# Kernel: packed attention into a mixture of experts, where the opening is re-ordered (second half of the first batch's tokens, identity matmuls, second batch's attention)

## The chip, the cores and the metric

The kernel runs on one core of one Trainium2 chip. The metric is the device time of one execution in microseconds; lower is better. The median of three runs of the kernel before is 1284.36 us, from 1283.30 to 1284.87.

## What is computed

Attention in two steps, eight batches of eight heads, 576 positions and 64 columns a head: 32 packed queries `p` attend to `k` and `v`, then `q` attends to what they found. The result is the input of a mixture of four experts with given weights.

```python
p_packed = sm_attn(p, k, v)            # (8, 8, 32, 64)
out = sm_attn(q, p_packed, p_packed)   # (8, 8, 576, 64)
x = out.transpose(0, 2, 1, 3).reshape(4608, 512)
p = domain_probs / (domain_probs.sum(-1, keepdims=True) + 1e-09)
for e in range(4):
    h = np.maximum(x @ w1[e], 0.0)     # 512 -> 1024
    y += p[:, e:e + 1] * (h @ w2[e])   # 1024 -> 512
```

## The kernel before, in words

**Tokens.** The attention weights of the second step have only 32 columns a head, so `x @ w1` is computed as (weights `a2`) times (`p_packed @ w1`). `pack_unit` (L176) makes `p_packed` of a batch and leaves it in `ppbd`: scores on TensorE, row maximum on VectorE, exponential on ScalarE, transposes with the identity, product with `v`. The weights `a2`, transposed, are the tokens `xh` and `xl`, a high and a low part in fp32r: ScalarE writes `xh` (a rounding copy), GpSimd writes `xl` (the remainder). For the first batch `tok_halves` (L292) does this for positions 0 to 287 and 288 to 575 apart, each for two groups g of four heads; for all others `tok_unit` (L256) does whole rows. In `tok_halves`, `shifted` subtracts the maximum and calls for the exponential, and `normed` sums, inverts, multiplies, transposes (five VectorE instructions) and makes `xh` and `xl`.

**Chunks and units.** The 4 x 1024 hidden columns are eight chunks `ch` of 512. A unit is one chunk of one batch: `units` lists (0, 0, 0), (0, 1, 0), (0, 1, 1), (0, 0, 1) and so on as (pair of batches, chunk, batch), so units 0 and 1 are the first batch's and unit 2 the first of the second batch. `g_form` (L359) makes `ghl`, the product of `ppbd` with a piece of `w1`, for a chunk (8 matmul calls a batch). `mm1_group(u, kh, c)` (L403) makes one quarter block of the hidden layer of unit u: token half c, hidden half kh, named a11, a12, a21, a22 (`f"a{c + 1}{kh + 1}"`), 24 x 128x288 matmuls for two blocks; one VectorE SCALAR_TENSOR_TENSOR does the ReLU and the weight.

**Seven products.** The second layer is a 2 x 2 block product done with seven products in the order `ORDER` (a11, s3, s1, s2, a22, s4, a12). `mm1_group` forms the sums s1 to s4 on VectorE; `s_operand` (L453) makes the high part of an operand `st` on ScalarE and the low part on GpSimd; a12's own operand `stl` has its low part made on VectorE, out of PSUM. `product` (L516) is 12 matmuls; its result is copied to `acc` by ScalarE (first chunk of a batch) or added by VectorE. `t_form` (L485) makes the weights `tt` of a chunk out of two pieces `rw0` and `rw1` of `w2`: four subtractions on GpSimd (in place in `rw`), high parts on ScalarE, low parts on GpSimd. The next chunk's pieces are loaded into the same tiles by SyncE once the last low part was read.

**Memory for sums.** PSUM holds four tiles `dbl` of two banks; nearly every step on TensorE takes one, so a tile that is read late holds up a later step.

**What sets the order.** Engines take their instructions in a fixed order. A scheduler puts it together when the kernel is built; the code constrains it: `together` and `on_pe` (L96 to L118) chain TensorE, `InOrder` keeps VectorE and GpSimd in the order of the code while `on` is set (from L659 to L683), and `Behind` puts attention work of VectorE (`avec`) behind the latest block sum. `avec.on` also keeps matmuls of other kinds behind the latest product (L99), from unit 1 on.

**The opening.** L641 to L684 are the code before the units: first batch's attention, `halves` in steps, `g_form` of chunk 0, weights of chunk 0 in steps (`forms`), second batch's score matmuls (`packs[2:]`), then blocks a11 and a12 (`mm1_group(0, 0, 0)`, `(0, 1, 0)`), which need the first half of the tokens, and a22 and a21, which need the second. The loop over units (L708) then issues, after each product i, the operands, `g_form`, blocks of the next unit, and one or two steps of `second_batch` (L688), which was drained before unit 1.

## Time and profile before

| | |
|---|---|
| median of three runs | 1284.36 us (1283.30 to 1284.87) |
| the profiled execution | 1284.25 us |
| its span, first to last instruction | 1282.5 us |
| outside the span | 1.75 us |
| TensorE (PE) busy | 1247.8 us, 97% of the span |
| VectorE (DVE) busy | 926.9 us, 72% |
| GpSimd (POOL) busy | 729.5 us, 57% |
| ScalarE (ACT) busy | 501.5 us, 39% |
| mean granted clock of TensorE | 0.996 |

How to read the views: a row of the timeline gives start and duration in us, the engine, the line, the operation, what it writes and reads, the count, and in square brackets the idle time before it with what ended that. A row that stands for several instructions runs from the first one's start to the last one's end. PE are matmuls, PEld weight loads, SPq the issue of transfers by SyncE. In a row of the windows the stretch comes first, then its length, the busy time of PE, PEld, DVE, ACT and POOL with their counts, the granted clock, the share of the transfer engines and GB/s. A group's row ends with the count, busy time, mean ns of one, and the idle time before.

### The profile page before, as it was taken

How to read it: one execution, taken by the hardware profiler on the slowest of the kernel's cores; microseconds unless marked ns; L12 is line 12 of the kernel's file. 1: busy time of each engine (PE TensorE's matmuls, PEld its weight loads, DVE VectorE, ACT ScalarE, POOL GpSimd, SP SyncE). 2: the span in 40 equal slices, each digit the busy share in tenths (PEclk: the TensorE clock that was granted, in tenths of full speed). 3: DMA queues.
4: the chain of work that ended last, by engine and by line, in shares of the span. 5: the costliest groups of instructions: out<-in, count | busy, mean ns of one | idle time of the engine just before them, and what ended most of it. 6: DMA issues, size and time to landing. Idle time of an engine off the chain costs nothing.

```text
span 1282.5 us, 26863 instructions
## 1 busy us (share of the span) xinstructions
PE 1247.8 (97%) x10720; PEld 1165.6 (91%) x10720; DVE 926.9 (72%) x1398; ACT 501.5 (39%) x850; POOL 729.5 (57%) x528
## 2 busy tenths in 40 slices
PE   5899999999999999999999999999999999999997
PEld 3789998988989999999999999999999999999997
DVE  6675776697975677889685666788768467766677
ACT  2555544344445343334235433343333533333331
POOL 3877868778774343455466343454457445434545
PEclk9899999999999999999999999999999999999999
DMA  9675656425465444554454554433445443344422
GB/s 339 237 259 172 231 200 242 170 102 209 160 222 181 159 157 165 158 168 152 132 171 153 180 191 160 157 118 117 158 153 198 151 136 118 129 135 158 125 66 75
DMA packets 86220, 213.71 MB, mean 167 GB/s; under 512 B 8784, under 2 KB 27344, under 8 KB 86096
## 3 DMA queue, kind: packets, MB, share of 16 engines
q1 hardware_dynamic: 85424, 211.85, 49.4%
q8 instruction: 86, 1.41, 0.5%
q14 instruction: 38, 0.31, 0.1%
q10 hardware_dynamic: 672, 0.15, 0.1%
HBM read 173.09 MB, written 38.87 MB: 165 GB/s over the span
## 4 chain that ended last, share of the span: by engine, by line
PE 82%; POOL 5%; DVE 5%; DMA 3%; issue 3%; ACT 1%; POOLq 0%; SPq 0%; DVEq 0%; ACTq 0%
PE dbl L104 76%; PE dbl L112 5%; POOL st L68 3%; DVE acc L68 1%; POOL acc L68 1%; DVE a L68 1%; POOL tt L68 1%; DMA rw<-in_w 1%; DMA pnd<-ablk 1%; PE dbl L107 1%; DVE ghl L68 1%; DMA pbt<-pnd 1%; POOL rw L68 0%; DVE dbl L68 0%; DVE sblk L68 0%
## 5 line engine op out<-in xcount | busy, mean ns | idle before, releaser
L104 PE MATMUL dbl<-st,tt 128*128 128x288 f32 x4608 | 665.9, 296 | 11.0 <-POOL st L68 6.5
L104 PEld LDWEIGHTS dbl<-st,tt 128*128 128x128 f32 x4608 | 622.9, 188 | 46.5 <-issue 27.2
L68 POOL TENSOR_TENSOR st<-sblk,st 128x576 fp32r<-128x576 f32 x256 | 373.3, 1468 | 391.2 <-ACT st L139 364.3
L104 PE MATMUL dbl<-xh,ghl 128*128 128x288 f32 x2048 | 414.4, 295 | 0.0
L68 DVE TENSOR_TENSOR acc<-dbl,acc 128x576 f32<-128x576 f32 x391 | 293.3, 751 | 87.3 <-PE dbl L104 85.0
L104 PEld LDWEIGHTS dbl<-xh,ghl 128*128 128x128 f32 x2048 | 328.8, 189 | 0.2 <-DVE ghl L68 0.2
L104 PE MATMUL dbl<-xl,ghl 128*128 128x288 f32 x1024 | 303.0, 296 | 6.4 <-POOL xl L68 5.7
L139 ACT CAST st<-sblk 128x576 fp32r<-128x576 f32 x256 | 166.5, 674 | 310.7 <-DVE sblk L68 253.7
L68 POOL TENSOR_TENSOR st<-ablk,st 128x576 fp32r<-128x576 f32 x128 | 185.2, 1447 | 53.3 <-ACT st L139 51.1
L104 PEld LDWEIGHTS dbl<-xl,ghl 128*128 128x128 f32 x1024 | 193.1, 189 | 9.3 <-POOL xl L68 6.4
L68 DVE SCALAR_TENSOR_TENSOR dbl<-dbl,pbt 128x576 f32<-128x576 f32 x128 | 97.8, 764 | 83.3 <-PE dbl L104 77.0
L139 ACT CAST st<-ablk 128x576 fp32r<-128x576 f32 x128 | 86.2, 674 | 151.1 <-PE dbl L104 125.4
L68 DVE SCALAR_TENSOR_TENSOR ablk<-dbl,pbt 128x576 f32<-128x576 f32 x128 | 96.4, 753 | 49.6 <-PE dbl L104 46.7
L68 DVE TENSOR_TENSOR ghl<-dbl,ghl 128x512 fp32r<-128x512 f32 x128 | 85.3, 687 | 54.3 <-ACT ghl L139 54.3
L104 PE MATMUL dbl<-stl,tt 128*128 128x288 f32 x768 | 113.0, 296 | 1.0 <-DVE acc L68 1.0
L104 PEld LDWEIGHTS dbl<-stl,tt 128*128 128x128 f32 x768 | 104.4, 188 | 3.2 <-DVE acc L68 2.6
L139 ACT CAST ghl<-dbl 128x512 fp32r<-128x512 f32 x128 | 72.0, 588 | 60.5 <-DVE ghl L68 50.8
L68 POOL TENSOR_TENSOR tt<-rw,tt 128x512 fp32r<-128x512 f32 x56 | 71.9, 1300 | 33.4 <-ACT tt L139 33.3
L68 DVE TENSOR_TENSOR stl<-dbl,stl 128x576 fp32r<-128x576 f32 x64 | 48.3, 755 | 38.4 <-ACT stl L139 38.4
L112 PE MATMUL dbl<-wraw,ppbd 64*32 64x512 f32 x1024 | 67.5, 595 | 0.8 <-DMA wraw<-in_w 0.8
L440 ACT COPY sblk<-dbl 128x576 f32<-128x576 f32 x64 | 41.0, 641 | 66.5 <-DVE sblk L68 66.5
L533 ACT COPY acc<-dbl 128x576 f32<-128x576 f32 x56 | 35.9, 640 | 49.9 <-PE dbl L104 49.8
(63 smaller groups left out, 695.4 us busy)
## 6 DMA issues: line engine op xcount, KB each, us to landing
tt<-td SPq DMA_DIRECT2D x175, 512.0 KB, 4.2
wraw<-in_w SPq DMA_DIRECT2D x132, 256.0 KB, 3.7
td<-tt SPq DMA_DIRECT2D x56, 512.0 KB, 5.2
pbt<-pnd SPq DMA_DIRECT2D x32, 288.0 KB, 3.8
out<-acc SPq DMA_DIRECT2D x32, 288.0 KB, 2.6
rw<-in_w SPq DMA_DIRECT2D x16, 512.0 KB, 5.8
kt<-in_k SPq DMA_DIRECT2D x14, 576.0 KB, 6.0
kt<-in_q SPq DMA_DIRECT2D x14, 576.0 KB, 4.8
```

Source lines behind the costliest of these rows:

```text
L68: res = getattr(self.eng, op)(*args, **kw)
L104: on_pe(nc.tensor.matmul(**kw))
L107: on_pe(nc.tensor.transpose(**kw))
L112: ins = nc.tensor.matmul(**kw).ins
L139: nc.scalar.copy(out=dst, in_=src)
L440: nc.scalar.copy(out=held("s1"), in_=psv)
L533: nc.scalar.copy(out=accs[b, i], in_=psv)
```

## The change

Lines of the kernel before are meant where nothing else is said.

- **Tokens first.** The second half's first group (`normed(0, 1)`) is issued with the second half's `shifted`, ahead of block a11's ReLU, and the second group (`normed(1, 1)`) after a11 and ahead of a12's.
- **Identity matmuls.** `warm(16)`: 16 fp32 products of the 128 x 128 identity with itself, into a `dbl` tile that nobody reads, between blocks a12 and a22.
- **a12 of unit 0** goes to SBUF (a third `ablk` tile) and its operand is made as any other, by `s_operand`, with the low part on GpSimd.
- **Weights.** The subtractions t1 and t2 of chunk 0 stand one step later; chunk 1's first two steps come after product 2, not 0 and 2; chunk 1's four subtractions go to VectorE (`avec`).
- **g_form of unit 0** (chunk 1) comes after product 1, not 0.
- **Second batch.** `second_batch` gets 2, 2, 2, 2, 1, 1 steps in unit 0 and up to 12 after the first three products of unit 1; before it was drained ahead of unit 1. The rules on order (`avec.on`, `strict`) hold from unit 0, and VectorE keeps the code's order from product 5 of unit 0 to product 2 of unit 1.

VectorE at the end of the opening, before: `ablk` is block a11, `a_338` and `a_339` are the second half's two groups, `at` their transposes.

```order
L68 TENSOR_TENSOR a_339<-a_339,m_424 128x288
L68 SCALAR_TENSOR_TENSOR ablk<-dbl,pbt 128x576
L68 TENSOR_REDUCE s_453<-a_338 128x9
L68 TENSOR_SCALAR s_453<-s_453 128x9
L68 RECIPROCAL s_453<-s_453 128x9
L68 TENSOR_TENSOR a_338<-a_338,s_453 128x288
L68 STREAM_TRANSPOSE at<-a_338 128x288
L68 TENSOR_REDUCE s_461<-a_339 128x9
L68 TENSOR_SCALAR s_461<-s_461 128x9
L68 RECIPROCAL s_461<-s_461 128x9
L68 TENSOR_TENSOR a_339<-a_339,s_461 128x288
```

VectorE at the same place, now:

```order
L69 TENSOR_TENSOR a_339<-a_339,m_430 128x288
L69 TENSOR_REDUCE s_434<-a_338 128x9
L69 TENSOR_SCALAR s_434<-s_434 128x9
L69 RECIPROCAL s_434<-s_434 128x9
L69 TENSOR_TENSOR a_338<-a_338,s_434 128x288
L69 STREAM_TRANSPOSE at<-a_338 128x288
L69 SCALAR_TENSOR_TENSOR ablk<-dbl,pbt 128x576
L69 TENSOR_REDUCE s_458<-a_339 128x9
L69 TENSOR_SCALAR s_458<-s_458 128x9
L69 RECIPROCAL s_458<-s_458 128x9
L69 TENSOR_TENSOR a_339<-a_339,s_458 128x288
```

The first group's five instructions moved ahead of a11's SCALAR_TENSOR_TENSOR, the second group's behind it.

ScalarE in unit 0, before: `acc` are product results, `ghl` chunk 1 of `g_form`, `rw_557` the second weights' piece, `at` the second batch's transposes.

```order
L139 CAST ghl<-dbl 128x512
L440 COPY sblk<-dbl 128x576
L139 CAST ghl<-dbl 128x512
L139 CAST st<-sblk 128x2x288 x2
L139 CAST st<-ablk 128x2x288
L231 COPY at<-dbl 128x512
L232 COPY at<-dbl 64x128
L533 COPY acc_638<-dbl 128x576
L139 CAST st<-sblk 128x2x288
L231 COPY at<-dbl 128x512
L232 COPY at<-dbl 64x128
L139 CAST tt<-rw_557 128x512
```

ScalarE at the same place, now (the piece is `rw_572`):

```order
L449 COPY sblk<-dbl 128x576
L140 CAST st<-sblk 128x2x288 x2
L140 CAST st<-ablk 128x2x288
L140 CAST tt<-rw_572 128x512
L544 COPY acc_632<-dbl 128x576
L140 CAST st<-sblk 128x2x288
L140 CAST ghl<-dbl 128x512 x2
L232 COPY at<-dbl 128x512
L233 COPY at<-dbl 64x128
```

The rounding copy of the new weights' piece stood behind the copies to `ghl` and `at` and the second product's `acc`; it stands ahead of them now.

VectorE in unit 1, before, from the second batch's multiplications (`a_781`, `a_793`) to its first transpose:

```order
L68 TENSOR_TENSOR a_781<-a_781,s_867 128x576
L68 TENSOR_TENSOR sblk<-dbl,sblk 128x576
L68 TENSOR_TENSOR a_793<-a_793,s_872 128x576
L68 TENSOR_TENSOR acc_574<-dbl,acc_574 128x576
L68 STREAM_TRANSPOSE at<-a_781 128x576
L68 TENSOR_TENSOR ghl<-dbl,ghl 128x512
L68 TENSOR_TENSOR stl<-dbl,stl 128x2x288
L68 TENSOR_TENSOR ghl<-dbl,ghl 128x512
L68 TENSOR_TENSOR acc_638<-dbl,acc_638 128x576
```

VectorE there now, behind `stl` of unit 1 (the second batch's tiles are `a_796`, `a_808`):

```order
L69 TENSOR_TENSOR acc_589<-dbl,acc_589 128x576
L69 TENSOR_TENSOR ghl<-dbl,ghl 128x512 x2
L69 TENSOR_REDUCE s_971<-a_796 128x18
L69 TENSOR_SCALAR s_971<-s_971 128x18
L69 RECIPROCAL s_971<-s_971 128x18
L69 TENSOR_TENSOR a_796<-a_796,s_971 128x576
L69 TENSOR_TENSOR acc_632<-dbl,acc_632 128x576
L69 TENSOR_REDUCE s_996<-a_808 128x18
L69 TENSOR_SCALAR s_996<-s_996 128x18
L69 RECIPROCAL s_996<-s_996 128x18
L69 TENSOR_TENSOR a_808<-a_808,s_996 128x576
L69 STREAM_TRANSPOSE at<-a_796 128x576
```

The sums, reciprocals and multiplications of the second batch stood ahead of `stl` and of the chunk's `ghl`; they stand behind both now, and behind one product's sum more.

The diff, without the two lines that only rename:

```diff
@@ -34,6 +34,7 @@
 
 ORDER = ["a11", "s3", "s1", "s2", "a22", "s4", "a12"]
 NPROD = len(ORDER)
+WARM = 16
 
 
 @with_exitstack
@@ -90,13 +91,13 @@
                 return res
             return issue
 
-    order["sum"], order["product"] = None, None
+    order.update(sum=None, product=None, strict=False)
     vec, avec = Behind(vq, None), Behind(vq, "sum")
 
     def on_pe(res):
         if order["last"] is not None:
             after(res.ins, order["last"])
-        if avec.on and order["product"] is not None:
+        if order["strict"] and order["product"] is not None:
             after(res.ins, order["product"])
         order["free"].append(res.ins)
 
@@ -340,9 +341,9 @@
         yield
         for g in range(NG):
             shifted(g, 1)
-        yield
-        for g in range(NG):
-            normed(g, 1)
+        normed(0, 1)
+        yield
+        normed(1, 1)
         yield
 
     def w1_load(ch):
@@ -400,6 +401,13 @@
 
     blocks = {}
 
+    def warm(n):
+
+        ps = dbl()
+        together([
+            dict(out=ps[:, 0, 0:P], lhsT=ident, rhs=ident, start=True, stop=True) for _ in range(n)
+        ])
+
     def mm1_group(u, kh, c):
         sb, ch, b = units[u]
         xh, xl = xs[b]
@@ -428,8 +436,9 @@
             vec.tensor_tensor(out=dst, in0=x, in1=y, op=op)
 
         name = f"a{c + 1}{kh + 1}"
+        early = name == "a12" and (u, "a22") not in blocks
         vec.scalar_tensor_tensor(
-            out=held(name) if c == kh else psv, in0=psv, scalar=0.0,
+            out=held(name) if c == kh or early else psv, in0=psv, scalar=0.0,
             in1=pbt[b][:, ts].rearrange("p (o t) -> p o t", o=1).broadcast_to([P, 2, HS]),
             op0=ALU.max, op1=ALU.mult,
         )
@@ -443,8 +452,8 @@
         elif name == "a12":
             if (u, "s2") in blocks:
                 add(held("s4"), psv, blocks[u, "s2"], ALU.subtract)
-            else:
-                blocks[u, "a12"] = psv
+            if early:
+                return
             st = hpool.tile([P, 2, 2, HP], F32R, name="stl")[:, :, :, 0:HS]
             hi_of(st[:, 0], psv, nc.scalar)
             lo_of(st[:, 1], psv, st[:, 0], vec)
@@ -482,7 +491,7 @@
     def raw_tile(shape, name):
         return wpool.tile(shape, F32, name=name)
 
-    def t_form(ch, first=False):
+    def t_form(ch, first=False, eng=gq):
 
         raw = [w2r.pop((ch, kh)) for kh in range(2)]
         blk = {
@@ -493,6 +502,8 @@
         steps = (
             ("a11", "t1", "t3"), ("s3", "s1", "t2"), ("s2", "t4"), ("a22",), ("s4",), ("a12",),
         )
+        if first:
+            steps = steps[:1] + (("s3", "s1"), ("t2",)) + steps[2:]
         how = {"t1": ("b12", "b11", "b11"), "t2": ("b22", "t1", "t1"), "t3": ("b22", "b12", "b12"), "t4": ("t2", "b21", "t2")}
         for names in steps:
             for name in names:
@@ -504,7 +515,7 @@
             for name in names:
                 if name in how:
                     x, y, place = how[name]
-                    gq.tensor_tensor(out=blk[place], in0=blk[x], in1=blk[y], op=ALU.subtract)
+                    eng.tensor_tensor(out=blk[place], in0=blk[x], in1=blk[y], op=ALU.subtract)
                     blk[name] = blk[place]
                 else:
                     t = tt[ch, ORDER.index(name)]
@@ -669,12 +680,14 @@
             next(gen)
         next(halves)
         drain(fold)
+        next(forms)
         next(halves)
         next(forms)
         mm1_group(0, 0, 0)
+        next(halves)
         s_operand(0, 0)
-        next(halves)
         mm1_group(0, 1, 0)
+        warm(WARM)
         for gen in packs[2:]:
             next(gen)
         mm1_group(0, 1, 1)
@@ -700,20 +713,19 @@
     GROUPS = {1: ((0, 0),), 3: ((1, 1),), 4: ((0, 1),), 6: ((1, 0),)}
     GROUPS_FIRST = {2: ((0, 0),), 3: ((1, 1),), 4: ((0, 1),), 6: ((1, 0),)}
     GROUPS_LATE = {3: ((0, 0),), 4: ((1, 1),), 5: ((0, 1),), 6: ((1, 0),)}
-    FORM = {0: (0, 2, 3, 4, 5, 6), 2: (6,), 3: (0, 1, 2, 3, 4)}
+    FORM = {0: (2, 2, 3, 4, 5, 6), 2: (6,), 3: (0, 1, 2, 3, 4)}
     for kh in range(2):
         w2_load(1, kh, raw_tile)
     tsteps = nothing
     sums, back = nothing, second_batch()
+    avec.on = order["strict"] = True
+    order["product"] = order["free"][-1]
     for u, (sb, ch, b) in enumerate(units):
         pos = u % (2 * NCH)
         odd = pos % 2 == 1
         opening = u < 4
         nxt = units[u + 1] if u + 1 < len(units) else None
 
-        if u == 1:
-            drain(back)
-            avec.on = True
         if sb + 1 < SB and pos == (4 if sb == 0 else 1):
             drain(back)
             back = pair_attention([2 * sb + 2, 2 * sb + 3])
@@ -722,7 +734,7 @@
         gsteps, gat = nothing, (2, 3)
         nsb, nch = (sb, ch + 1) if ch + 1 < NCH else (sb + 1, 0)
         if u == 0:
-            gsteps, gat = g_form([0], 1, raws), (0,)
+            gsteps, gat = g_form([0], 1, raws), (1,)
         elif u == 1:
             gsteps, gat = g_form([1], 1, raws), (0,)
         elif u == 2:
@@ -731,7 +743,7 @@
             gsteps = g_form([2 * nsb, 2 * nsb + 1], nch, raws)
         fch = {0: 1, 2: 2, 3: 2}.get(u, ch + 1 if u > 3 and sb == 0 and ch + 1 < NCH else None)
         if fch is not None and u != 3 and not (u > 3 and odd):
-            tsteps = t_form(fch)
+            tsteps = t_form(fch, eng=gq if u else avec)
         form_at = FORM.get(u, () if fch is None else (1, 2, 3, 4) if odd else (1, 4))
         for i in range(NPROD):
             product(u, i)
@@ -741,7 +753,7 @@
             elif nxt:
                 s_operand(u + 1, n - NPROD)
             if i in gat:
-                if gat == (0,):
+                if len(gat) == 1:
                     drain(gsteps)
                     if 0 < u < 4:
                         raws = w1_load({1: 0, 2: 2}[u])
@@ -754,11 +766,17 @@
                     mm1_group(u + 1, *grp)
             if i == 4 and 2 <= u < len(units) - 2 and units[u + 2][1] % 2 == 0:
                 load_probs(units[u + 2][2], units[u + 2][1] // 2)
-            if i in slots:
+            if u == 0:
+                for _ in range(2 if i < 4 else 1 if i < 6 else 0):
+                    next(back, None)
+            elif u == 1:
+                for _ in range((1, 2, 9, 0, 0, 0, 0)[i]):
+                    next(back, None)
+            elif i in slots:
                 next(back, None)
-                if u == 0:
-                    next(back, None)
-            if i in form_at:
+            if (u, i) in ((0, 5), (1, 2)):
+                vq.on, vq.last = u == 0, None
+            for _ in range(form_at.count(i)):
                 next(tsteps, None)
             if u == 1 and i < 2:
                 w2_load(2, i, raw_tile)
```

## The prediction

> **What bounds the kernel now.** I read the page first: busy time of TensorE, its busy share in 40 slices, the chain that ended last.
>
> ```profile
> PE 1247.8 (97%) x10720; PEld 1165.6 (91%) x10720; DVE 926.9 (72%) x1398; ACT 501.5 (39%) x850; POOL 729.5 (57%) x528
> PE   5899999999999999999999999999999999999997
> PE 82%; POOL 5%; DVE 5%; DMA 3%; issue 3%; ACT 1%; POOLq 0%; SPq 0%; DVEq 0%; ACTq 0%
> ```
>
> TensorE is the bound, and it is short of work only in the first slices. So a change in the opening is worth what it does to the moment from which TensorE is full, and that moment is moved one to one into the end if nothing later gives it back. Next, the windows say where that moment is, and TensorE's waits up to 110 us, of which the longest is shown, what is lost ahead of it.
>
> ```profile
> 34.20:40.20 6.00, 5.89 (x21) 5.22 (x22) 4.13 (x11) 3.58 (x8) 4.85 (x5) 0.50 0.93 368
> 72.60:250.00 177.40, 176.19 (x1589) 163.12 (x1590) 118.15 (x188) 80.06 (x141) 132.98 (x101) 1.00 0.58 198
> PE dbl L104 <- POOL xl L68: 5.7, 1, 5.7
> ```
>
> From 72.6 to 250 us TensorE idles 1.2 us of 177.4: there is no slack that could take up a delay. In the stretch behind the longest wait the granted clock is 0.50. TensorE's timeline has the marks that I use below: blocks a11 and a12, a22 and a21 (`xl,ghl`), product a11 (x12), `g_form` of chunk 1 (x16), product s3 (x12), the second batch's two products with `v` (`xl,at`), the last `g_form` of unit 0, unit 1's products s3, s1, s2 (x36), unit 2's first block.
>
> ```profile
> 24.97 0.37 PE L104 MATMUL dbl<-xl,ghl 128*128 128x288 f32 x1 [0.34 <-DVE ghl L68]
> 34.18 0.61 PE L104 MATMUL dbl<-xl,ghl 128*128 128x288 f32 x1 [5.67 <-POOL xl L68]
> 40.65 1.74 PE L104 MATMUL dbl<-st,tt 128*128 128x288 f32 x12
> 42.32 1.92 PE L112 MATMUL dbl<-wraw,ppbd 64*32 64x512 f32 x16
> 45.78 1.82 PE L104 MATMUL dbl<-st,tt 128*128 128x288 f32 x12
> 47.53 0.90 PE L104 MATMUL dbl<-xl,at 128*32 128x64 f32 x40
> 49.39 0.65 PE L104 MATMUL dbl<-xl,at 128*32 128x64 f32 x32 [0.95 <-ACT at L231]
> 68.92 1.92 PE L112 MATMUL dbl<-wraw,ppbd 64*32 64x512 f32 x16
> 72.64 4.97 PE L104 MATMUL dbl<-st,tt 128*128 128x288 f32 x36 [1.79 <-DVE acc L68]
> 77.45 0.30 PE L104 MATMUL dbl<-xl,ghl 128*128 128x288 f32 x1
> ```
>
> A matmul of a product comes every (1.74 - 0.30) / 11 = 0.131 us, the last row's 0.30 being the length of one. The 24 of a22 and a21 would take 3.14 us; they took 40.65 - 34.18 = 6.47 at the half clock, so the slow clock cost 3.3. With the waits in brackets, 5.67 + 0.95 + 1.79, that is 11.7 us: about the most that the opening could give.
>
> **The change, part by part. 1: tokens ahead of the blocks.**
>
> ```profile
> 26.86 0.46 DVE L68 TENSOR_TENSOR a<-a,m 128x288 f32<-128x288 f32 x1
> 28.04 0.76 DVE L68 SCALAR_TENSOR_TENSOR ablk<-dbl,pbt 128x576 f32<-128x576 f32 x1 [0.71 <-DMA pbt<-pnd]
> 28.71 0.44 DVE L68 TENSOR_REDUCE s<-a 128x9 f32<-128x288 f32 x1
> 31.39 0.48 DVE L68 STREAM_TRANSPOSE at<-a 128x288 f32<-128x288 f32 x1
> 33.51 0.48 DVE L68 STREAM_TRANSPOSE at<-a 128x288 f32<-128x288 f32 x1
> 34.53 0.80 POOL L68 TENSOR_TENSOR xl<-at,xh 128x288 fp32r<-128x288 f32 x1 [0.41 <-ACT xh L139]
> ```
>
> The first group's five instructions took 31.87 - 28.71 = 3.16 us, the second's 33.99 - 31.87 = 2.12. Begun at 27.32, where VectorE is free, the first group ends between 29.4 and 30.5, a11's ReLU 0.7 later, the second group at 32.3 to 34.4; the first `xl` is there 1.3 after its group (34.53 + 0.80 - 33.99), so at 30.7 to 31.8, the second at 33.6 to 35.7. Before, the first matmul ran at 34.18.
>
> **2: identity matmuls.** No row shows such a one. The `wraw` row at 42.32 has 16 records of 512 columns in 1.92 us with four side by side (64*32 tiles), so 0.48 alone, 0.12 for 128 columns; 16 fp32 products are 32 records (each fp32 call shows two), 3.8 us. The least is that of the narrow `xl,at` records, 32 x 0.90 / 40 = 0.7. I take 3.8, since that row has fp32 operands of full width. Their tile must be free: four `dbl` tiles are in use, and a11's goes at its ReLU, 30.1 to 31.2. They end at 34 to 35, and a22 and a21 follow at full clock: 37.1 to 38.2 instead of 40.65, 2.5 to 3.5 earlier. The page "TensorE: Matmul & The Clock Gate" of the Trainium skill, Part 1, says that an idle window of about 3.4 us halves the clock; the trace agrees, with 0.50 behind a wait of 5.67. By that rule the change wins the 3.3 us whole, and with nothing late behind it the time would be 1284.25 - 3.3 = 1281.0.
>
> **3: what is late next: GpSimd.** The groups of GpSimd (20 to 80 us):
>
> ```profile
> L68 POOL TENSOR_TENSOR tt<-rw,tt 128x512 fp32r<-128x512 f32 x13 | 16.7, 1305 | 2.4 <-ACT tt L139 2.4
> L68 POOL TENSOR_TENSOR rw<-rw,rw 128x512 f32<-128x512 f32 x6 | 8.2, 1364 | 0.5
> L68 POOL TENSOR_TENSOR st<-ablk,st 128x576 fp32r<-128x576 f32 x4 | 5.9, 1472 | 0.1
> L68 POOL CAST tt<-rw 128x512 fp32r<-128x512 f32 x4 | 2.6, 666 | 0.1
> L68 POOL TENSOR_TENSOR xl<-at,xh 128x576 fp32r<-128x576 f32 x2 | 2.9, 1426 | 1.2 <-ACT xh L139 1.2
> 43.71 1.41 POOL L68 TENSOR_TENSOR st<-sblk,st 128x576 fp32r<-128x576 f32 x1 [0.67 <-ACT st L139]
> ```
>
> Behind the second `xl` (33.6 to 35.7) it has a11's `st`, a cast, a low part, a subtraction, a cast and three low parts of chunk 0: 1.47 + 2 x 0.67 + 1.36 + 4 x 1.31 = 9.4, so 43.0 to 45.1. Only then comes s3's `st`, 1.41: product s3 can start at 44.4 to 46.5. Before it started at 45.78, with `g_form` (1.92) already done; now `g_form` is behind it. TensorE's lead is spent, and it stands 0.5 to 2.6 behind. The four subtractions of chunk 1 that go to VectorE (4 x 1.36 freed) stood behind this place and don't help here.
>
> **4: what is late next: ScalarE.**
>
> ```profile
> rw<-in_w SPq DMA_DIRECT2D x1, 512.0 KB, 5.7
> 43.06 0.38 SPq L479 DMA_DIRECT2D rw<-in_w  x1
> L139 ACT CAST tt<-rw 128x512 fp32r<-128x512 f32 x9 | 5.2, 619 | 3.7 <-POOL rw L68 3.7
> L533 ACT COPY acc<-dbl 128x576 f32<-128x576 f32 x7 | 4.5, 637 | 5.4 <-PE dbl L104 5.4
> L139 ACT CAST st<-sblk 128x576 fp32r<-128x576 f32 x8 | 5.2, 681 | 0.7 <-POOL st L68 0.7
> L139 ACT CAST ghl<-dbl 128x512 fp32r<-128x512 f32 x4 | 2.4, 593 | 0.0
> L231 ACT COPY at<-dbl 128x512 f32<-128x512 f32 x2 | 1.2, 602 | 0.0
> ```
>
> The piece of `w2` is issued when GpSimd has read the old one, at 43.06 before and about then now, and lands 5.7 later, 48.8. ScalarE's copy of it now stands ahead of product s3's `acc`, of both `ghl` and of the second `at`: a new wait of some 5 us. `acc` is copied at 48.8 + 0.62 + 0.64 = 50.1 and frees the tile of the first product with `v` (47.53 before); `st`, two `ghl` and two `at` (0.68 + 1.19 + 0.60 + 0.26) put the second at 52.5 at the most. I take 51.9, since these copies follow each other a little closer than their lengths: 2.5 behind 49.39, with 1.5 to either side for the issue.
>
> **5: the rest of unit 0.** TensorE has the same instructions from there, so its last `g_form` ends at 70.84 + 2.5 = 73.3. VectorE has the four subtractions more; by the group below 1.0 us each (1.108 x 512 / 576), by the `ghl` row 0.66; it hides them, being idle between TensorE's steps.
>
> **6: the second batch reaches into unit 1.** VectorE's groups (57 to 76 us):
>
> ```profile
> L68 DVE TENSOR_TENSOR a<-a,s 128x576 f32<-128x576 f32 x2 | 2.2, 1108 | 0.0
> L68 DVE TENSOR_TENSOR acc<-dbl,acc 128x576 f32<-128x576 f32 x2 | 1.5, 740 | 0.0
> L68 DVE TENSOR_REDUCE s<-a 128x18 f32<-128x576 f32 x2 | 1.5, 736 | 0.0
> L68 DVE TENSOR_TENSOR ghl<-dbl,ghl 128x512 fp32r<-128x512 f32 x2 | 1.3, 657 | 0.0
> L68 DVE STREAM_TRANSPOSE at<-a 128x576 f32<-128x576 f32 x1 | 0.8, 761 | 0.0
> ```
>
> Now `stl` and the two `ghl`, which wait for that `g_form`, stand ahead of the second batch's sums. ScalarE's `ghl`, exponential and `stl` end about 1.9 behind `g_form` (three of 0.6 to 0.7, as the casts of part 4), 75.2; VectorE's `stl` at 75.9 frees TensorE's next tile: products s3, s1, s2 run from 75.9 to 80.9 instead of 72.64 to 77.6. VectorE then does `acc`, two `ghl`, twice (sum, two short ones of about 0.35, multiplication), one `acc`, the transpose: 0.74 + 1.31 + 2 x 2.55 + 0.74 + 0.76 = 8.65. The short ones' 0.35 is an estimate from part 1's second group (2.12 less 0.44, 0.48 and some 0.5 for the multiplication, halved). Where the next needs no result it starts 0.09 early (28.04 + 0.76 - 28.71); seven of these leave 8.0. With ScalarE's `xh` (as a cast of `st`, 0.68) and GpSimd's `xl`, 1.43, the tokens are there at 86.0. TensorE's order has unit 2's block behind product s2, so it waits from 80.9 to 86.0, and starts at 86.0 what it started at 77.45: **8.6 later**. Nothing behind it gives that back (1.2 us of idle up to 250 us).
>
> **7: the clock behind that wait.** 5.1 us is little less than the 5.67 that cost 3.3; what it costs lies between 0 and 3.3, and I take 2.0. By the rule on windows cited in part 2, which runs freely, half of such waits (1.7 of 3.4) would hold a whole idle window, and the cost would be 1.7. In the earlier hole ahead of s3 a slow clock costs nothing, since TensorE waits for ScalarE behind it anyway.
>
> **Sum.** 1284.25 for the profiled execution (span 1282.5 and 1.75 around it; the median of the runs is 0.11 above) + 8.6 + 2.0 = 1294.9 us.
>
> **Rivals.** *The opening's gain survives* (faster). If unit 1's second product starts before 72.64, part 1 and 2 keep what they earn, 3.0 in the middle: 1281.3. For it speaks that TensorE's longest wait and its slow clock do go (the rule of the Trainium skill in part 2 speaks for the same); against it, that GpSimd's row up to 43.04 is full already and that the fixed orders of ScalarE and VectorE put landings and `g_form` ahead. *The second batch is late, but TensorE hardly waits for it*: the new wait of part 4 holds, 2.5 to 3.3, and VectorE's chain is short enough, which it is if the sums of part 6 take 5 us less: 1287.2. *The identity matmuls come too late for the clock*: 3.3 more on a22 and a21, hidden behind GpSimd's 43.0: the forecast's time. *Both waits go cold and the landing is late*: over 1298.7.
>
> **How the numbers follow.** Forecast, 1290.3 to 1298.7 (part 4 to 6 by 2.5 less and the clock at 0; 2.5 more and the clock at 3.3): 0.74. Second rival and what lies between it and the forecast, 1287 to 1290: 0.10. More than 1298.7: 0.04. Faster: 0.08. Within 0.2% (2.6 us, about what a measurement of this kernel can tell from no change), the lead and the loss in balance: 0.04. So faster 0.08, same 0.04, slower 0.88. The range 1288.5 to 1299.0 leaves out the first and last cases and a half of the second rival.
>
> **What would show it.** Right: no wait of TensorE for `xl` near 28 to 34 and granted clock 1.00 there; product s3 at 44 to 46; ScalarE idle up to 48 or 49 with the landing of `rw` as its end; `g_form` of unit 0 ending at 72 to 75; one wait of about 5 us for `xl` at 80 to 87, with clock 0.50 behind it or not. Wrong: TensorE full from 73 on, or the wait at 81 under 2 us.

## The result, and the profile after

| | before | after |
|---|---|---|
| median of four runs | 1284.61 us (1283.30 to 1285.92) | 1298.76 us (1297.51 to 1300.03) |
| ratio | | 1.0104, 95% interval 1.0091 to 1.0117 |
| profiled execution, its span | 1284.25, 1282.5 us | 1298.29, 1296.5 us |

The change makes the kernel slower by 1%. The page of the kernel after, with TensorE's busy time, its busy share in 40 slices and the chain that ended last:

```profile
PE 1252.7 (97%) x10752; PEld 1170.6 (90%) x10752; DVE 931.9 (72%) x1401; ACT 501.8 (39%) x850; POOL 725.3 (56%) x525
PE   6779999999999999999999999999999999999997
...
PE 75%; POOL 10%; DVE 4%; issue 4%; DMA 4%; ACT 1%; POOLq 0%; DVEq 0%; SPq 0%; ACTq 0%
```

The first slice is fuller than before (6 against 5), because 1.1 us of identity matmuls fall into it; the second and third are emptier (7 and 7 against 8 and 9). In the chain GpSimd's share has doubled, 5% to 10%. Windows over the stretch with the identity matmuls and blocks a22 and a21, and over the two with a low clock behind it (columns as in the prediction):

```profile
31.33:38.30 6.97, 6.97 (x57) 6.88 (x58) 5.60 (x11) 2.75 (x6) 5.52 (x6) 1.00 1.02 392
43.90:50.72 6.82, 3.77 (x16) 3.10 (x20) 0.00 (x0) 1.45 (x3) 6.82 (x6) 0.50 0.89 290
...
88.27:95.10 6.83, 5.63 (x23) 5.63 (x24) 1.81 (x3) 0.67 (x1) 2.56 (x2) 0.50 0.01 2
```

Blocks a22 and a21 now run at full clock; two later stretches have the half clock. The wait of 5.7 us for `xl` near 30 us is gone, and two about as long, 5.83 and 5.29, stand in its place. TensorE's timeline has them:

```profile
31.33 3.84 PE L113 MATMUL dbl<-ident 128*128 128x128 f32 x32 [2.42 <-DVE ablk L69]
...
38.30 1.74 PE L105 MATMUL dbl<-st,tt 128*128 128x288 f32 x12
...
46.95 3.25 PE L105 MATMUL dbl<-st,tt 128*128 128x288 f32 x12 [5.83 <-POOL st L69]
50.13 2.18 PE L113 MATMUL dbl<-wraw,ppbd 64*32 64x512 f32 x16
...
54.75 0.65 PE L105 MATMUL dbl<-xl,at 128*32 128x64 f32 x32 [1.14 <-ACT at L232]
...
74.28 1.92 PE L113 MATMUL dbl<-wraw,ppbd 64*32 64x512 f32 x16
...
79.21 4.98 PE L105 MATMUL dbl<-st,tt 128*128 128x288 f32 x36 [3.01 <-DVE stl L69]
89.47 0.61 PE L105 MATMUL dbl<-xl,ghl 128*128 128x288 f32 x1 [5.29 <-POOL xl L69]
```

Against before, product a11 starts 2.35 us earlier (38.30, 40.65), s3 1.17 later (46.95, 45.78), the second product with `v` 5.4 later (54.75, 49.39), the last `g_form` of unit 0 5.4 later, unit 1's products 6.6 later (79.21, 72.64), unit 2's block 12.0 later (89.47, 77.45). Behind it come some 2.4 us of slow clock (below), and the span is 14.0 longer. The rows of GpSimd, SyncE, ScalarE and VectorE behind these steps:

```profile
41.31 4.24 POOL L69 TENSOR_TENSOR tt<-rw,tt 128x512 fp32r<-128x512 f32 x3 [0.58 <-ACT tt L140]
45.52 4.12 POOL L69 TENSOR_TENSOR st<-sblk,st 128x576 fp32r<-128x576 f32 x3
...
45.58 0.38 SPq L488 DMA_DIRECT2D rw<-in_w  x1
...
51.51 0.62 ACT L140 CAST tt<-rw 128x512 fp32r<-128x512 f32 x1 [6.16 <-DMA rw<-in_w]
...
78.30 0.76 DVE L69 TENSOR_TENSOR stl<-dbl,stl 128x576 fp32r<-128x576 f32 x1 [1.62 <-ACT stl L140]
...
86.46 0.77 DVE L69 STREAM_TRANSPOSE at<-a 128x576 f32<-128x576 f32 x1
```

GpSimd reads chunk 0's weights for the last time until 45.55; only then is the piece of `w2` issued that ScalarE's next cast needs, and that cast holds all of ScalarE's row for 6.16 us. In unit 1 VectorE's sums and transpose of the second batch end at 87.23, behind `stl`.

### The profile page after: what moved, and what is told of

The parts are those of the page before. It is cut to its first block, busy times and chain, and to the rows that moved or that the text cites. A ratio compares the mean times of both kernels' runs of the same rounds, so it can differ in the third digit from the quotient of the medians.

```text
span 1296.5 us, 26932 instructions
## 1 busy us (share of the span) xinstructions
PE 1252.7 (97%) x10752; PEld 1170.6 (90%) x10752; DVE 931.9 (72%) x1401; ACT 501.8 (39%) x850; POOL 725.3 (56%) x525
## 3 DMA queue, kind: packets, MB, share of 16 engines
q1 hardware_dynamic: 85424, 211.85, 48.8%
## 4 chain that ended last, share of the span: by engine, by line
PE 75%; POOL 10%; DVE 4%; issue 4%; DMA 4%; ACT 1%; POOLq 0%; DVEq 0%; SPq 0%; ACTq 0%
PE dbl L105 70%; PE dbl L113 5%; POOL st L69 5%; POOL tt L69 2%; DMA rw<-in_w 2%; POOL rw L69 1%; POOL acc L69 1%; DVE acc L69 1%; DVE a L69 1%; DMA tt<-td 1%; DVE ghl L69 1%; PE dbl L108 1%; DMA wraw<-in_w 0%; DVE s L69 0%; ACT tt L140 0%
## 5 line engine op out<-in xcount | busy, mean ns | idle before, releaser
L69 POOL TENSOR_TENSOR tt<-rw,tt 128x512 fp32r<-128x512 f32 x56 | 73.3, 1324 | 33.8 <-ACT tt L140 30.1
```

The source lines that it names most:

```text
L69: res = getattr(self.eng, op)(*args, **kw)
```

## Experiments

**Theory.** The loss is made of three late orders: GpSimd's full row ahead of s3; ScalarE's cast, which waits for the landing, ahead of the second batch's steps; and in unit 1 the second batch's sums behind `stl` on VectorE, with the slow clock behind that wait. **Rivals.** The identity matmuls cost it (3.8 us of TensorE and a tile); VectorE's four more subtractions, or the late `g_form`, cost it. The kernels were run in three groups, each on one chip with the kernel before beside it (medians 1285.2, 1286.4 and 1285.6 us there), so the ratio to before is what compares them; 0.1% is 1.3 us. The changed kernel stands at 1.0104.

**1. The second batch ended ahead of unit 1.**

```diff
-    avec.on = order["strict"] = True
-    order["product"] = order["free"][-1]
...
+        if u == 1:
+            drain(back)
+            avec.on = order["strict"] = True
...
-                for _ in range(2 if i < 4 else 1 if i < 6 else 0):
-                    next(back, None)
-            elif u == 1:
-                for _ in range((1, 2, 9, 0, 0, 0, 0)[i]):
+                for _ in range(2):
                     next(back, None)
...
-            if (u, i) in ((0, 5), (1, 2)):
-                vq.on, vq.last = u == 0, None
```

> The changed kernel, with the second batch's attention ended ahead of unit 1 as before (all of step 6 undone; the opening, the identity matmuls, the late g_form and the subtractions on VectorE stay). Theory of three late orders: the opening's loss stays (last product with v near 54.8, +5.4; last g_form of unit 0 ends near 76.2), the wait for xl at 84 goes, and with it the half clock behind it; unit 2's block near 77.45 + 5.4 = 82.9, time 1284.3 + 5.4 = 1289.7, between 1288.5 and 1291.5. Rival, the identity matmuls cost the time: nothing of them is undone, 1298. Rival, VectorE's four more subtractions cost it: undone neither, 1297 to 1298.

Measured: 1292.99 us, ratio 1.0053 (1.0033 to 1.0073), so some 6.5 us of the 13.4 go. The wait for `xl` is gone. The 1289.7 was missed, and the timelines of TensorE, GpSimd and VectorE show two places:

```profile
32.02 5.47 PE L113 MATMUL dbl<-ident 128*128 128x128 f32 x32 [2.72 <-DVE ablk L69]
...
58.48 0.90 PE L105 MATMUL dbl<-xl,at 128*32 128x64 f32 x40 [2.47 <-issue]
...
43.50 4.24 POOL L69 TENSOR_TENSOR tt<-rw,tt 128x512 fp32r<-128x512 f32 x3 [2.12 <-ACT tt L140]
...
55.90 1.87 DVE L69 TENSOR_TENSOR rw<-rw 128x512 f32<-128x512 f32 x1 [10.52 <-POOL tt L69]
57.70 0.68 DVE L69 TENSOR_TENSOR ghl<-dbl,ghl 128x512 fp32r<-128x512 f32 x1
```

In this profile the identity matmuls ran partly at the half clock (5.47 instead of 3.84; why is told under the clock, at the end); product a11, ScalarE's copy of it and the casts behind that copy came later, GpSimd waited 2.12 for them instead of 0.58, and product s3 came at 49.14 instead of 46.95. And VectorE's order, another one now, has a subtraction of chunk 1 ahead of `ghl`: `ghl` ends at 58.38, its tile is free, and TensorE's second product with `v` starts at 58.48, after a hole that the profile puts to no one ("issue").

**2. Two casts from GpSimd to ScalarE.**

```diff
-                hi_of(t[:, 0], blk[of[name]], gq if first and of[name][0] == "t" else nc.scalar)
+                hi_of(t[:, 0], blk[of[name]], gq if first and name in ("s3", "s1") else nc.scalar)
```

> The changed kernel, with two casts of chunk 0 (s2 and a22, 0.61 us each) on ScalarE, which is idle there, instead of GpSimd. Theory of three late orders: GpSimd's row up to its last low part ends 1.2 earlier (44.3 instead of 45.55), product s3 starts 1.2 earlier, the piece of w2 is issued and lands 1.2 earlier, and so all behind it: at least 1.2 off the end, 1297.1, and if the shorter wait ahead of s3 keeps the clock at 1.00 up to 3 more, 1294 to 1297. Rivals (identity matmuls, or VectorE's subtractions, set the end): 1298.3, give or take 0.5, since neither waits for GpSimd.

Measured: 1293.64 us, 1.0062 (1.0045 to 1.0078), 5.4 less than the changed kernel, more than the 1.2 to 4.3 expected. The timeline of SyncE, ScalarE and TensorE:

```profile
41.39 0.38 SPq L488 DMA_DIRECT2D rw<-in_w  x1
...
45.88 0.62 ACT L140 CAST tt<-rw 128x512 fp32r<-128x512 f32 x1
...
45.75 3.13 PE L105 MATMUL dbl<-st,tt 128*128 128x288 f32 x12 [3.13 <-POOL st L69]
```

Product s3 starts 1.2 earlier, as expected. What was not: GpSimd's order of the last three low parts came out another way, the piece that the cast needs is now the first of two to be issued, at 41.39 instead of 45.58, lands 4.5 later, and nothing waits for it. TensorE has its second product with `v` at 52.28. So the run took away 1.2 us of GpSimd's delay and ScalarE's wait for the landing together, and their shares can't be told apart by it.

**3. The wait in unit 1 filled.**

```diff
+            if (u, i) == (1, 3):
+                warm(20)
```

> The changed kernel, with 20 more identity matmuls put in TensorE's wait for the second batch's tokens, behind product s2 of unit 1 (some 4.8 us of TensorE's time; their result is read by nobody). Theory of three late orders: unit 2's block starts at the same time (89.5, since it waits for xl), at granted clock 1.00 instead of 0.50: 2.5 to 3.3 off, 1295.0 to 1295.8; this is step 7's term by itself. Rival, identity matmuls take time from TensorE that it needs: slower, 1298.3 + up to 4.8.

Measured: 1296.79 us, 1.0090 (1.0065 to 1.0114): 1.8 less by the ratios, under the 2.5 to 3.3 expected, and not to be told from the changed kernel by the time alone. The windows do tell; first the changed kernel, then this one:

```profile
90.00:100.00 10.00, 10.00 (x60) 10.00 (x59) 3.26 (x5) 1.34 (x2) 2.37 (x2) 0.75 0.00 0
```

```profile
90.00:100.00 10.00, 10.00 (x78) 10.00 (x77) 5.67 (x8) 1.94 (x3) 3.10 (x3) 1.00 0.01 2
```

TensorE is busy throughout in both, with 60 matmuls in one and 78 in the other. At 0.131 us a matmul, 18 more are 2.4 us: that is the clock's term, counted from 90 us on. Put into a wait, 20 more identity matmuls made the kernel not slower.

**4. No identity matmuls.**

```diff
-        warm(WARM)
```

> The changed kernel without the 16 identity matmuls; a22 and a21 then run at the clock that the waits for the two xl leave. Theory of three late orders: GpSimd's row and the landing set the opening's end either way, so 1296.5 to 1299. Rival, the identity matmuls (3.8 us of TensorE and a PSUM tile) cost the time: 1294.5 or less.

Measured: 1297.95 us (1294.72 to 1300.17), 1.0093 (1.0070 to 1.0116). No gain that can be told; but the interval reaches to 4.4 us less than the changed kernel, so this run does not exclude the rival's 3.8. It does show that most of the 13.4 us are not theirs. The waits moved, as the timelines of ScalarE and TensorE show:

```profile
54.98 0.62 ACT L140 CAST tt<-rw 128x512 fp32r<-128x512 f32 x1 [6.59 <-DMA rw<-in_w]
...
56.28 1.82 PE L105 MATMUL dbl<-st,tt 128*128 128x288 f32 x12 [3.52 <-ACT acc L544]
...
86.57 0.61 PE L105 MATMUL dbl<-xl,ghl 128*128 128x288 f32 x1 [5.28 <-POOL xl L69]
```

GpSimd's order came out another way here too: product s3 starts at 43.06, and the wait for the landing holds up a later `acc`. This profile is of the fastest run of four (1294.72); in it unit 2's block starts 2.9 earlier than in the changed kernel's.

**5 and 6. The front alone, and with the cast later.** Of the change only the opening is left (tokens first, identity matmuls, a12 kept, t1 and t2 a step later): experiment 1's edit, and

```diff
-            gsteps, gat = g_form([0], 1, raws), (1,)
+            gsteps, gat = g_form([0], 1, raws), (0,)
...
-            tsteps = t_form(fch, eng=gq if u else avec)
+            tsteps = t_form(fch)
...
-    FORM = {0: (2, 2, 3, 4, 5, 6), 2: (6,), 3: (0, 1, 2, 3, 4)}
+    FORM = {0: (0, 2, 3, 4, 5, 6), 2: (6,), 3: (0, 1, 2, 3, 4)}
```

Experiment 6 adds one order on ScalarE, where `order["at"]` is the second of the two copies `at` of a batch:

```diff
+                if ch == 1:
+                    after(cast, order["at"])
```

> Of the change only the opening's part is left: tokens ahead of a12 and a22, a12 kept early, the identity matmuls, the split step of chunk 0. The second batch ends ahead of unit 1, g_form and chunk 1's first step stand behind product 0, the four subtractions are on GpSimd, as before. Theory of three late orders: GpSimd's row still ends near 45.5 and ScalarE's cast of the landing piece still stands ahead of acc of product s3 and the second at, so the opening's loss stays, 5.4: 1289.7, between 1288 and 1292 (the clock over the identity matmuls is worth 2). Rival, the loss comes from what reaches into units 0 and 1 (subtractions on VectorE, late g_form, second batch): 1282 to 1284.5.

> The kernel with the front alone, and one order more: ScalarE's first casts of chunk 1, which wait for the landing of w2, stand behind the second batch's second at. Theory of three late orders: TensorE no longer waits for the landing; product s3 starts near 46 to 47 (45.78 before), the second product with v near 50.5: 1284.3 + 1.2 = 1285.5, between 1284 and 1288, 3 to 5 less than with the cast ahead. Rival, GpSimd's row or the identity matmuls alone set the loss: no change from the front alone.

Measured: 1294.25 us, 1.0064 (1.0049 to 1.0079), and 1288.01 us, 1.0022 (1.0010 to 1.0034). One order on ScalarE is worth 0.42%, 5.4 us. ScalarE and TensorE with the cast ahead, then behind:

```profile
52.66 0.62 ACT L140 CAST tt<-rw 128x512 fp32r<-128x512 f32 x1 [5.17 <-DMA rw<-in_w]
...
54.92 0.73 PE L105 MATMUL dbl<-xl,at 128*32 128x64 f32 x32 [2.47 <-ACT at L232]
```

```profile
54.14 0.62 ACT L140 CAST tt<-rw 128x512 fp32r<-128x512 f32 x1
...
54.14 0.65 PE L105 MATMUL dbl<-xl,at 128*32 128x64 f32 x32 [0.76 <-ACT at L231]
```

TensorE's wait shrinks from 2.47 to 0.76. The marks of experiment 6 came later than expected (s3 at 49.26 instead of 46 to 47, the second product with `v` at 54.14 instead of 50.5); the time, 1287.1 by its ratio, lies in the expected range. The front alone was 2.8 us above the 1289.7 even by its ratio (1292.5). The identity matmuls were slow in both profiles, but that of the front alone has one more wait, of 3.6 us, far behind the edit. TensorE's waits from 230 to 520 us and VectorE's timeline, front alone, then VectorE with the cast later:

```profile
PE dbl L105 <- DVE acc L69: 4.3, 3, 3.6
...
266.44 5.56 DVE L69 TENSOR_TENSOR a<-a,m 128x576 f32<-128x576 f32 x1
```

```profile
263.52 1.57 DVE L69 TENSOR_TENSOR a<-a,m 128x576 f32<-128x576 f32 x1
```

VectorE's order is the same at that place; the one subtraction, which `acc` stands behind, took 5.56 instead of 1.57 beside GpSimd (below, last part). Of the profiles only this one and experiment 11's have that, so it need not be in every run. Of the 5.4 us, the rows near the edit account for 3.2: unit 1's products start at 77.35 instead of 80.56. The rest need not be the cast's.

**7. The front without identity matmuls.** Experiment 5's kernel without `warm(WARM)`.

> The kernel with the front alone, without the 16 identity matmuls. The order that comes out then has ScalarE's casts of the landing piece behind the second at, as before. Theory of three late orders: like the front with the cast later, less the slow clock's share, 1282 to 1286. Rival, that identity matmuls matter by TensorE's time: 3.8 less than the front alone.

Measured: 1287.68 us, 1.0015 (1.0003 to 1.0028), 6.3 less than the front alone; 1286.2 by its ratio, just above the expected range. In its order ScalarE's cast does stand behind the second `at`, and s3's operand ahead of chunk 0's last low parts on GpSimd. The time is not to be told from experiment 6, which leaves all of the identity matmuls in and moves the cast alone. So with the cast out of the way, leaving them out makes no difference that can be told; that the order which comes out with them is what costs is argued from this, not shown apart.

**8. The front with two casts on ScalarE.** Experiment 5's kernel with experiment 2's edit.

> The kernel with the front alone, and the two casts of chunk 0 (s2, a22) on ScalarE instead of GpSimd. Theory of three late orders: GpSimd's row ends 1.2 earlier, product s3 starts near 44.5; the order of ScalarE that comes out has the cast of the landing piece behind the second at; the opening's gain of some 1.3 survives: 1283, between 1281.5 and 1285.5. Rival, identity matmuls or the tokens' place cost the time whatever GpSimd does: 1288 or more.

Measured: 1285.94 us, 1.0001 (0.9990 to 1.0011). The loss is gone, and the expected gain of 1.3 did not come. TensorE's timeline:

```profile
46.02 2.62 PE L105 MATMUL dbl<-st,tt 128*128 128x288 f32 x12 [1.76 <-POOL st L69]
```

It still waits for GpSimd ahead of s3, and in unit 1 (products at 74.70) it waits 2.49 for GpSimd where before it waited 1.79 for VectorE.

**9. The cast later, alone.** The changed kernel with experiment 6's order.

> The changed kernel with one order more: ScalarE's first casts of chunk 1, which wait for the landing of w2, stand behind the second batch's second at (they stood ahead of acc, both ghl and that at). Everything else stays. Theory of three late orders: product s3 still near 47, but the second product with v at 51.5 to 52.5 instead of 54.75, and 1.5 to 3 off the end if the wait of step 6 is passed on unchanged: 1295.5 to 1297. Rival, the landing is hidden by GpSimd's row: no change.

Measured: 1295.46 us, 1.0080 (1.0060 to 1.0100), 3.1 less than the changed kernel by the ratios, whose intervals overlap a little. TensorE and ScalarE:

```profile
53.71 0.65 PE L105 MATMUL dbl<-xl,at 128*32 128x64 f32 x32 [0.70 <-ACT at L231]
...
53.71 0.62 ACT L140 CAST tt<-rw 128x512 fp32r<-128x512 f32 x1
```

ScalarE no longer waits for a landing. TensorE gains 1.0 here, not the 2 to 3 expected: s3 still came at 46.81, at the slow clock, and `g_form` stands behind it. Unit 2's block starts 1.75 earlier (87.72). The wait for `xl` ahead of it is 3.15 instead of 5.29, but 1.4 of that is no gain: unit 1's three products ran partly at half clock, in 6.40 instead of 4.98. The time is about what was expected, by other parts than expected.

**10. Experiment 1 with the subtractions on GpSimd** (`t_form(fch)` in the place of `t_form(fch, eng=gq if u else avec)`).

> The kernel with the second batch ended ahead of unit 1 (1293.0 when it ran), with chunk 1's four subtractions back on GpSimd. If the idle 2.5 us ahead of the second product with v came from a subtraction of 1.87 us that stood ahead of both ghl on VectorE: that hole shrinks to 1.1, and 1 to 3 come off, 1290 to 1292. Rival, it came from something else on TensorE: the hole stays, 1293.

Measured: 1292.44 us, 1.0049 (1.0033 to 1.0066), above the 1290 to 1292 expected and not to be told from experiment 1 by its time. The hole is 1.13 instead of 2.47, so the subtraction did make it:

```profile
55.02 0.65 PE L105 MATMUL dbl<-xl,at 128*32 128x64 f32 x32 [1.13 <-ACT at L232]
```

Experiment 5 is this kernel with `g_form` and chunk 1's first step back behind product 0. Its ratio is no lower (1.0064), though a late wait told there may be in it. So no run shows by its time that the late `g_form` costs.

**11. All three orders back**: the edits of experiments 1, 2 and 6 in the changed kernel.

> The changed kernel with all three late orders undone, each by itself as in the runs above: the second batch ends ahead of unit 1, two casts of chunk 0 on ScalarE, the casts of the landing piece behind the second at. Tokens first, the identity matmuls, the late g_form, chunk 1's first steps behind product 2 and the subtractions on VectorE stay. Theory of three late orders: of the 14 us some 3 to 5 are left, for subtractions and g_form: 1287.5 to 1289.5. Rival, the rest of the change costs more than that: over 1291.

Measured: 1291.47 us, 1.0042 (1.0027 to 1.0058). The rival's side: 8 of the 13.4 us go and 5.4 stay. Three things stay in the rows of TensorE and VectorE. TensorE still waits for GpSimd ahead of s3, so that order is undone only in part; `g_form` stands between s3 and the products with `v`, where before it filled the wait ahead of s3; and there is a new wait for a block's ReLU, which VectorE has behind one of the subtractions:

```profile
45.78 3.25 PE L105 MATMUL dbl<-st,tt 128*128 128x288 f32 x12 [4.64 <-POOL st L69]
48.96 2.81 PE L113 MATMUL dbl<-wraw,ppbd 64*32 64x512 f32 x16
...
62.69 0.40 PE L105 MATMUL dbl<-xl,ghl 128*128 128x288 f32 x1 [2.21 <-DVE ablk L69]
...
60.09 1.88 DVE L69 TENSOR_TENSOR rw<-rw,rw 128x512 f32<-128x512 f32 x1 [3.28 <-POOL tt L69]
61.89 0.74 DVE L69 SCALAR_TENSOR_TENSOR ablk<-dbl,pbt 128x576 f32<-128x576 f32 x1
```

So VectorE's subtractions are not free; in the changed kernel longer waits hid them. This profile is of the slowest run of five (1296.48 us), 5.0 above the median. It has the late wait of experiment 5's profile too (VectorE's subtraction took 5.56 again, TensorE waited 3.59 at 274.07, with 6.8 us of half clock about it), which the other four need not have. So its rows show where time goes, not how much goes in the median run.

**12. The lightest GpSimd row that was tried**: the front with experiments 2's and 6's edits, and the low parts of the operands of s3 and s1 on VectorE.

```diff
-        lo_of(st[:, 1], src, st[:, 0], gq)
+        lo_of(st[:, 1], src, st[:, 0], vec if u == 0 and i in (1, 2) else gq)
```

> The front alone, with the casts of chunk 0 on ScalarE, the casts of the landing piece behind the second at, and the low parts of the operands of s3 and s1 on VectorE instead of GpSimd (two of 1.41 us). Theory of three late orders: GpSimd is off the path ahead of s3, which starts near 44; second product with v near 49; the identity matmuls' gain of clock survives: 0.5 to 2.5 less than before, 1283 to 1285 where before takes 1285.5. Rival, the opening is bound elsewhere: as before.

Measured: 1285.52 us, 1.0004 (0.9993 to 1.0015): as before, as the rival had it. GpSimd is off the path ahead of s3 (TensorE's timeline), but s3 starts at 46.45, now behind VectorE's `ghl`, and in unit 1 the products start at 74.00, after 2.48 of wait for GpSimd:

```profile
46.45 1.85 PE L105 MATMUL dbl<-st,tt 128*128 128x288 f32 x12 [1.16 <-DVE ghl L69]
```

No kernel here beats the one before.

## Why the prediction was right, and where its terms were off

The direction and the mechanism held. The size was short: 14.0 us in the profiled execution (1298.3) where 10.6 were forecast (1294.9), and the median, 1298.76, lies inside the range by only 0.24 (1299.0 the upper end). What happened is nearer to the last rival, both waits cold and the landing late, over 1298.7, which had been given 0.04. By its parts:

- **1 and 2 held.** The identity matmuls took 3.84 us (3.8 forecast; a nearer row than that of `wraw` was there, ten 128x128 products with the identity at 44.71 in 1.31 us, so 4.2 for 32); a22 and a21 ended at 38.3 (37.1 to 38.2), at a clock of 1.00. That the clock was 1.00 was in part luck: in five other kernels here a wait about as long ahead of the identity matmuls halved it (last part). The rule of the Trainium skill's page "TensorE: Matmul & The Clock Gate", Part 1, agrees with the clock of this profile, a wait of 2.42 us being shorter than its window, but not with those five, where waits of 2.7 us halved it; the 1281.0 us that the rule would give with nothing late behind did not come, because GpSimd was late.
- **3 held as a mechanism; both times lie 0.45 behind its ranges.** GpSimd's last low part ended at 45.55 (43.0 to 45.1) and s3 started at 46.95 (44.4 to 46.5): 0.58 of wait for ScalarE's casts was not in the sum, and one of the last three low parts took 1.78, not 1.31, beside VectorE's sum s4 (last part).
- **4 is the step that failed, in size.** It took the issue of the piece "at 43.06 before and about then now". That is the end of the row which part 3 had just put at 43.0 to 45.1; the issue can't come before it. It came at 45.58, the landing 5.9 later at 51.5 instead of 48.8, and the second product with `v` at 54.75 instead of 51.9: 2.85 us. ScalarE's cast did hold up TensorE as described (experiments 6 and 9). But it was not the only thing: with the cast out of the way (experiment 9) the second product with `v` still came at 53.71, 1.8 behind the 51.9, because s3 ran at the half clock (3.25 us instead of 1.82) with `g_form` (2.2) behind it. Part 7 had put the slow clock in that hole at nothing, which is so only while the landing is later still. The sum of the five copies, too, makes 52.8, not the 52.5 "at the most".
- **5** carried these 2.9 on: `g_form` ended at 76.20, not 73.3. That VectorE hides the subtractions holds for the changed kernel, with TensorE late for other reasons. Experiments 1 and 11 show them ahead of `ghl` and of a ReLU, where TensorE waits for them.
- **6 held.** From unit 1's products to unit 2's block it had 86.0 - 75.9 = 10.1 us; the trace has 89.47 - 79.21 = 10.26. Its start was 3.3 late: 2.9 by part 4 and 0.4 of its own.
- **7**: 2.0 forecast, 2.4 by experiment 3's count of matmuls.

Sum: 12.0 for unit 2's block (8.6 forecast) and 2.4 for the clock (2.0) make 14.4, of which 14.0 arrive at the end.

Of the rivals, "the opening's gain survives" asked that unit 1's second product start before 72.64; no kernel here did that, not even those with GpSimd relieved. The second rival, that TensorE hardly waits for the second batch, is out: it waited 5.29. The third, the identity matmuls too late for the clock, did not come true in this profile. The theory of three orders as the whole of it is not shown: the second batch's is shown by the time (experiment 1), GpSimd's only together with the landing (2), the cast's by its rows, with a time at the edge of the noise (9); and with all three edits 5.4 us of 13.4 stay (experiment 11). Of these the trace shows the subtractions' 2.2 us, GpSimd's wait that is left and `g_form` on TensorE's path; how much each is worth, beside chunk 1's late first steps and the clock, is open.

## What to carry to other kernels

When an early wait of the bounding engine is removed, follow each queue that its work moved past to its last entry, and carry that very time into everything that starts behind it: a transfer into a tile that is used again starts when its last reader ends, not when it started before. An instruction that waits for a landing holds its whole in-order row, so what matters is what stands behind it. Orders that come out of a scheduler can change with any edit (experiments 2 and 4), so such an edit is not one change; a part that costs nothing behind a longer wait has to be costed again once that wait is gone. A profile is one run: a wait in it, far behind the edit, need not be in the others (experiments 5 and 11).

## What the runs showed of the hardware

**The clock.** Both slow stretches of the kernel after last 6.82 to 6.83 us (windows above), as does the one of before:

```profile
33.44:40.27 6.83, 5.98 (x22) 5.31 (x23) 4.86 (x13) 3.76 (x8) 5.61 (x6) 0.50 0.94 368
```

So a wait of 5 to 6 us is paid for with up to 6.8 us at half speed, less what of it is idle: in the stretch from 88.27 TensorE worked 5.63, which is 2.8 us lost at the most. The Trainium skill's page "TensorE: Matmul & The Clock Gate", Part 1, has windows of about 3.4 us that run freely, and one busy window to lift the clock; two windows are 6.83, and the trace agrees if the first, idle at its start, does not count as busy. A wait of 2.4 to 2.7 us ahead of the identity matmuls gave either clock: they took 3.84 us in six of the eleven kernels that have them and 5.46 or 5.47 in five. What decided is where the wait lay. Windows of experiment 1, then of the changed kernel, 3.41 us each and counted from an edge of the clock:

```profile
29.12:32.53 3.41, 0.69 (x6) 0.52 (x5) 3.27 (x7) 0.97 (x2) 2.04 (x3) 1.00 1.07 373
32.53:35.94 3.41, 3.41 (x18) 3.41 (x18) 3.31 (x6) 0.57 (x2) 2.04 (x3) 0.50 1.06 400
```

```profile
26.84:30.25 3.41, 2.06 (x16) 1.83 (x14) 3.24 (x7) 0.66 (x2) 2.97 (x3) 1.00 1.02 385
30.25:33.66 3.41, 2.33 (x20) 2.33 (x21) 3.27 (x7) 1.10 (x2) 2.02 (x2) 1.00 1.07 383
```

In experiment 1 the whole wait of 2.72 lies inside one window, TensorE is busy for 0.69 of its 3.41 us, and the next window runs at half clock; in the changed kernel the wait is split over two, and the clock stays. Counted like this, the wait lies inside one window in all five slow profiles (to 0.02 us) and is split in all six others. So a window need not be wholly idle, and a wait of 2.7 us can halve the clock.

**VectorE beside GpSimd.** A VectorE operation with two inputs in SBUF that began while GpSimd was in such a one was held until GpSimd's ended. VectorE's and GpSimd's timeline of the kernel after:

```profile
26.98 0.46 DVE L69 TENSOR_TENSOR a<-a,m 128x288 f32<-128x288 f32 x1
...
28.90 1.22 DVE L69 TENSOR_TENSOR a<-a,s 128x288 f32<-128x288 f32 x1
...
27.02 2.79 POOL L69 TENSOR_TENSOR tt<-rw,tt 128x512 fp32r<-128x512 f32 x2
```

The one at 28.90 ends at 30.12, 0.31 behind GpSimd's end at 29.81. The same shape took 0.46 us at 26.98, where it began 0.04 ahead of GpSimd's. The Trainium skill's page "GPSIMD Engine Reference", Specifications, says that the two engines share their SBUF interfaces, with contention for VectorE instructions that have two SBUF inputs; the trace agrees, and the price here is the rest of GpSimd's instruction. GpSimd pays as well: the low part that took 1.78 began at 42.53, while VectorE's sum s4 was under way (41.62 to 43.19), and that sum has two inputs in SBUF only because the change keeps a12 there.

The price can be several instructions. In experiment 5's profile VectorE's subtraction at 266.44 was held through four of GpSimd's that followed each other from 265.99 on, and ended 0.62 behind the last of them:

```profile
269.99 1.39 POOL L69 TENSOR_TENSOR st<-ablk,st 128x576 fp32r<-128x576 f32 x1
```

In experiment 6 the same subtraction, begun as far into the same GpSimd instruction (0.45 us), went ahead when that one ended, and GpSimd's next took 1.96 instead of 1.42. What decides between the two is not shown.
